# A transformer block in split precision: feature sums for two token tiles at a time in three buffers, one turn copied out of PSUM by ScalarE, and x loaded one item later

## The chip, the cores and the metric

The kernel runs on one core of a Trainium2 chip. The metric is the device time of one execution in microseconds; before the change its median over three runs is 1921.93 us (1920.83 to 1922.19). Engines are named as in the profile: PE (TensorE matmul) and PEld (its weight loads), DVE (VectorE), ACT (ScalarE), POOL (GpSimd) and SP (SyncE, which here only issues DMAs).

## What is computed

One pre-layer-norm block on x of 2048 tokens by 1024 channels, in float32, with 32 heads of 32 channels. Attention is linear, with learned softmax features:

```
h  = x + A(layernorm(x));  out = h + relu(layernorm(h) @ w1) @ w2

q, k, v = heads of layernorm(x) @ wqkv
phi_q = concat(softmax(q @ w_phi), softmax(-(q @ w_phi)))      # 64 features per head
phi_k = concat(softmax(k @ w_phi), softmax(-(k @ w_phi)))
kv = phi_k^T @ v;  z = sum over tokens of phi_k
A  = (phi_q @ kv) / (phi_q . z + 1e-6) @ wo
```

## The kernel before, in words

**Split precision.** Every large product is made of three matmuls, high by high, high by low and low by high (`mm3`, lines 180 to 183), on operands split into a high part (ACT, line 124 for weights) and a low part (DVE or POOL, line 128). PE takes four or eight such steps per item.

**The order.** The work is a list of items (`items`). Between the steps of the items, other functions run at fixed places: `do(n, k, f)` puts f behind step k of item n, `when(step, f)` behind a step counted through. Each function then adds its instructions to the queues of the engines that it names; an engine works through its own queue in that order, and what an instruction needs from another engine it waits for. So one late instruction holds all that stands behind it on its engine. The stages follow each other as: keys and values, queries, output product (`wo`), first MLP product (`up`), second one (`down`).

**The stretch around the change** is that from about 570 to 840 us: the last query items and the 32 items of the output product. Beside them runs the attention, in 32 units of four token tiles and eight heads (`UNITS`, line 524). For a unit u:

- `at_load` (528) loads the exponentials of the features, four tiles by 256 elements, into a tile `qe` (four buffers, two units of a pair in work and two ahead).
- `at_sums` (556): POOL multiplies them by the key sums z into `ez`, a tile of 128x1024 with one buffer (line 559).
- `at_reduce` (563): DVE sums `ez` over the features into `qtz` (line 565).
- `at_den` (571, POOL, lines 574 and 578), `at_inverse` (580, DVE, line 581) and `at_scale` (583, POOL, lines 591 and 596) make the features' scale and apply it.
- `at_turn` (599): DVE transposes in blocks (line 602).
- `at_num` (605), for two units at once: PE multiplies with the key-value sums into four PSUM banks, two named `tp` and two named `ac` (128 small matmuls, line 616); ACT copies them out as high parts (line 623), and `at_low` (632) has DVE make the low parts (line 634), with which the banks come free. The output product reads the result `oT`.

**Layer norm of h**, also beside the output product: `ln_pair` (675) takes two token tiles through nine stages. Stage 1 has DVE's statistics (line 220), stage 2 three POOL steps (229 to 231), stage 3 ACT's scaling (237). Stages 4, 5 and 6 turn a half tile each with four transposes on PE into a `tp` bank (line 244), which ACT copies out (246). Stage 7 turns the last half (line 697) into a `tp` bank, and DVE reads that bank twice, for a sum (698) and a difference (699). In stage 8, POOL makes two more differences (704, 705). `ln_store` sends seven halves off. This runs for b = 0 (four pairs, beside the output product) and for b = 1 (four pairs, beside the MLP).

**PSUM.** There are eight banks: four `mm`, two `tp`, two `ac`. The `tp` banks are handed out in turn, so that the four turns of a layer norm pair use them alternately, and the next `at_num` needs both.

**The residual.** `wo_load` (639) loads a half tile of x into `xh` (five buffers) two items before the item n that needs it (line 1030); `wo_add` (666) adds the product in place, `wo_store` (669) sends it off as h.

Of the kernel before, what the change touches and what calls it, by code (L numbers as in the profile page):

```python
# [9 lines left out]
F32 = mybir.dt.float32  # L10
F32R = mybir.dt.float32r
AF = mybir.ActivationFunctionType
ALU = mybir.AluOpType
AX = mybir.AxisListType

P = 128
S = 2048
D = 1024
H = 32
DH = 32  # L20
# [119 lines left out]
def kernel(  # L140
# [12 lines left out]
    v, act, pool, pe, sp = nc.vector, nc.scalar, nc.gpsimd, nc.tensor, nc.sync  # L153
# [12 lines left out]
    def tp_bank():  # L166
        return psum.tile([P, 512], F32, name="tp", bufs=2)
# [20 lines left out]
    def do(n, k, f, *args):  # L188
        at[n, k].append((f, args))
# [19 lines left out]
    def ln_load(key, parts):  # L209
        xin[key] = xlp.tile([P, D], F32, name="xl") if key[0] == "x" and key[1] >= HT and key[1] % 4 > 1 else \  # L210
            lnp.tile([P, D], F32, name="xin")
        n = D // len(parts)
        for j, p in enumerate(parts):
            sp.dma_start(xin[key][:, j * n:(j + 1) * n], p)

    def ln_stats(key):
        src = xin[key]
        st = lnp.tile([P, 2, 6], F32, name="st", bufs=4)
        for j in range(2):
            v.bn_stats(out=st[:, j, :], in_=src[:, j * 512:(j + 1) * 512])  # L220
        mv = lnp.tile([P, 2], F32, name="mv", bufs=4)
        v.bn_aggr(out=mv, in_=st)
        xst[key] = mv

    def ln_power(key):

        mv = xst[key]
        sc = scx[:, key[1] - HT, :] if key[0] == "s" else lnp.tile([P, 2], F32, name="sc", bufs=4)
        pool.tensor_scalar_add(sc[:, 0:1], mv[:, 1:2], LN_EPS)
        pool.tensor_tensor(out=sc[:, 0:1], in0=sc[:, 0:1], in1=half, op=ALU.pow)  # L230
        pool.tensor_scalar(sc[:, 1:2], mv[:, 0:1], sc[:, 0:1], -1.0, op0=ALU.mult, op1=ALU.mult)
        xst[key] = sc

    def ln_norm(key):
        sc, src = xst.pop(("s", key[1]) if key[0] == "x" and key[1] >= HT else key), xin.pop(key)
        xnt[key] = src if key[0] == "h" else fp_ln.tile([P, D], F32, name="xn")
        act.activation(xnt[key], src, AF.Identity, bias=sc[:, 1:2], scale=sc[:, 0:1])

    def ln_turn(key, j, dst=None):

        xn = xnt[key]
        pt = tp_bank().rearrange("p (k n) -> p k n", k=4)
        for k in range(4):
            pe.transpose(pt[:, k, :], xn[:, (4 * j + k) * P:(4 * j + k + 1) * P], ident)  # L244
        if dst is None:
            act.activation(xn[:, j * 512:(j + 1) * 512], pt.rearrange("p k n -> p (k n)"), AF.Copy)
            return
        d = dst()
        split(d[:, 0, 4 * j:4 * j + 4, :], d[:, 1, 4 * j:4 * j + 4, :], pt)
        if j == 1:  # L250
            del xnt[key]
# [269 lines left out]
    e_q, ez_of, tz_of, den_of, ph_of, acc_of, phT_of = {}, {}, {}, {}, {}, {}, {}  # L521
# [32 lines left out]
                           in1=den.rearrange("p (i h) -> p i h", i=4)[:, :, :, None].to_broadcast([P, 4, 4, 2]))  # L554

    def at_sums(u):
        b, q, r = UNITS[u]
        ez = ap_.tile([P, D], F32, name="ez", bufs=1).rearrange("p (i n) -> p i n", i=4)
        pool.tensor_tensor(out=ez, in0=e_q[u].rearrange("p (i h) s f -> p i (h s f)", i=4),  # L559
                           in1=zb[:, q, None, 256 * r:256 * (r + 1)].to_broadcast([P, 4, 256]), op=ALU.mult)  # L560
        ez_of[u] = ez

    def at_reduce(u):
        tz_of[u] = tz = ap_.tile([P, 32], F32, name="qtz", bufs=2)
        v.tensor_reduce(out=tz, in_=ez_of.pop(u).rearrange("p i (h f) -> p (i h) f", f=DH), op=ALU.add, axis=AX.X)

    def sm_half(u):
        b, q, r = UNITS[u]
# [68 lines left out]
    xh, wo_ps = {}, {}  # L637

    def wo_load(t, hf):
        xh[t, hf] = hp.tile([P, 512], F32, name="xh", bufs=5)  # L640
        sp.dma_start(xh[t, hf], x[t * P:(t + 1) * P, hf * 512:(hf + 1) * 512])

    def wo_item(t, hf, keys):
# [31 lines left out]
    def ln_pair(b, i, stage):  # L675

        keys = [("h", HT * b + 4 * r + i) for r in range(2)]
        if stage == 0:
            for key in keys:
                ln_load(key, [hd[key[1]]])  # L680
        elif stage == 1:
            for key in keys:
                ln_stats(key)
        elif stage == 2:
            for key in keys:
                ln_power(key)
        elif stage == 3:
            for key in keys:
                ln_norm(key)
        elif stage in (4, 5, 6):  # L690
            ln_turn(keys[stage // 6], stage != 4)
        elif stage == 7:
            x1, x2 = (xnt[key] for key in keys)
            s12 = (mp or hp).tile([P, 2, 512], F32, name="s12", bufs=1)
            pt = tp_bank()
            for k in range(4):
                pe.transpose(pt[:, k * P:(k + 1) * P], x2[:, k * P:(k + 1) * P], ident)
            v.tensor_add(s12[:, 0, :], pt, x2[:, 512:])
            v.tensor_sub(x2[:, 0:512], x1[:, 0:512], pt)
            sums[b, i] = s12  # L700
        elif stage == 8:
            x1, s12 = xnt[keys[0]], sums[b, i]
            s4 = (mp or hp).tile([P, 512], F32, name="s4l", bufs=1)
            pool.tensor_tensor(out=s12[:, 1, :], in0=s12[:, 0, :], in1=x1[:, 0:512], op=ALU.subtract)
            pool.tensor_tensor(out=s4, in0=x1[:, 512:], in1=s12[:, 1, :], op=ALU.subtract)
            sums[b, i] = s12, s4
# [127 lines left out]
    def item(gen, *args, keys):  # L834
        items.append((gen, args + (keys,)))
        steps.extend((k,) for k in keys)
        return len(items) - 1
# [10 lines left out]
    wo_first = len(items)  # L848
    for b, tiles in enumerate(groups):
        for hf in range(2):  # L850

            pairs = b == 0 and hf == 0
            for j in range(0, 4, 2 if pairs else 1):
# [3 lines left out]
                for half in range(2):  # L857
                    n = item(wo_pair, tiles[j:j + 2], hf, half, keys=[("wo", hf, 4 * half + k // 2) for k in range(8)])
# [26 lines left out]
    def when(step, f, *args):  # L885

        if step < 8 * first_up:
            do(step // 8, step % 8, f, *args)
        else:
            do(first_up + (step - 8 * first_up) // 4, step % 4, f, *args)  # L890
# [4 lines left out]
    for t in range(1, NT):  # L895
        n = t - 1 if t < HT else q_n[1, t - HT] + 1
# [25 lines left out]
    for n in range(1, 32):  # L922
        for k in ((6,) if n < 8 and n not in (3, 4, 5) else (2, 6)):
            if not todo:
                break
            p, kk = todo.pop(0)
# [68 lines left out]
    zb = kvL = smq = xlp = ap_ = hp = mp = dp = None  # L995
# [13 lines left out]
    for u in range(32):  # L1009
        start = 8 * (a0 + u) if u >= 8 else 8 * (last_kv + 4) + 19 * u // 2  # L1010
        slack = 6 if u < 6 else 0

        stages = (-8, 6, 10, 13, 16, 19, 25) if u < 12 else (7, 14, 18, 20, 22, 24, 28) if u % 2 == 0 else \
            (-1, 9, 13, 15, 17, 19, 23)
        for step, f in zip(stages, (at_load, at_sums, at_reduce, at_den, at_inverse, at_scale, at_turn)):
            if u >= EARLY or f in (at_load, at_scale, at_turn):
                when(max(start + step, 8 * (last_kv + 4)), f, u)
        if u % 2:
            when(start + 30 + slack, at_num, u)
            when(start + 32 + slack, at_low, u)  # L1020
        if u < EARLY:
            start = 8 * (kv_n[1, u // 2, NT - 1] + 4 + 4 * (u % 2))
            for step, f in ((0, early_load), (9, early_sums), (14, early_reduce), (16, at_den), (18, at_inverse),
                            (20, early_scale)):
                when(start + step, f, u)
# [1 line left out]

    order = sorted(wo_n.items(), key=lambda kv: kv[1])
    for (t, hf), n in order:
        do(max(n - 2, wo_first), -1, wo_load, t, hf)  # L1030
        when(8 * n + (11 if n < wo_first + 2 else 9), wo_add, t, hf)
        when(8 * n + (10 if n > order[-3][1] else 14), wo_store, t, hf)

# [5 lines left out]
    for i in range(4):  # L1039
        for stage in range(9):  # L1040
            when(wo0 + 64 + 40 * i + LN2[0][stage], ln_pair, 0, i, stage)
            when(up0 + 60 + 68 * i + LN2[1][stage], ln_pair, 1, i, stage)
        for j in range(7):
            when(wo0 + 64 + 40 * i + LN2[0][9] + j // 2, ln_store, 0, i, j)
            when(up0 + 60 + 68 * i + LN2[1][9] + j, ln_store, 1, i, j)
# [37 lines left out]
    for b in range(2):  # L1083
        for m in DOWN:
            n = down_n[b, m, NP - 1] + 1
            name, more = {1: "x1", 5: "x4", 6: "x2", 4: "x3"}.get(m), \
# [33 lines left out]
    for i in range(4):  # L1120
        r = slice(32 * i, 32 * (i + 1))
# [76 lines left out]
```

## Time and profile before

| | |
|---|---|
| median of three runs | 1921.93 us |
| the profiled execution | 1921.28 us |
| its span, from the first to the last instruction | 1919.4 us |
| mean granted TensorE clock | 0.997 |
| busy: PE, DVE, POOL, ACT | 1896.9, 1026.5, 967.6, 756.3 us |
| DMA, mean rate | 225 GB/s |

How to read it: the profile is of one execution. A row of the timeline has the start, the duration, engine, line, operation, output and inputs; in square brackets stands how long the engine was idle before it, and who ended that. A row of the waits has who waited for whom, the total, the number of times and the longest. A busy engine is not one at its peak: matmuls overlap each other, so the pace of PE is read from the distance between the starts of two of them.

### The profile page before, as it was taken

What the parts mean: (1) busy time and instruction counts of PE and PEld (TensorE: products, weight loads), DVE (VectorE), ACT (ScalarE), POOL (GpSimd) and SP (SyncE); (2) the same over time, 40 slices, a digit from 0 to 9 for tenths busy, and PEclk for the clock granted to TensorE, in tenths of its full rate; (3) what the DMA queues carried; (4) which work ended last, traced back from release to release, by engine and by line L of the source; (5) the groups of instructions that cost most, each with busy time, mean ns of one, the idle gap of its engine ahead of it and who ended that gap; (6) DMA issues with size and microseconds to landing.
All of it is one profiled execution on the core that took longest, in us unless ns stands there. A gap on an engine that the chain in (4) does not pass through costs nothing.

```text
span 1919.4 us, 31405 instructions
## 1 busy us (share of the span) xinstructions
PE 1896.9 (99%) x11416; PEld 1561.6 (81%) x11416; DVE 1026.5 (53%) x1631; ACT 756.3 (39%) x1310; POOL 967.6 (50%) x935
## 2 busy tenths in 40 slices
PE   9999999999999999999999999999999999999998
PEld 7888788877778777788888888888888888888887
DVE  6666578767679766545544564344433433343333
ACT  5433326222223112245444564444444444444442
POOL 4777752789955877423343322222244444444443
PEclk9999999999999999999999999999999999999999
DMA  6888786666665656697787897666677677777775
GB/s 219 276 264 271 231 275 198 209 196 211 192 218 182 204 206 235 204 285 225 247 265 237 255 295 221 187 185 193 212 243 226 191 240 233 242 212 220 215 216 170
DMA packets 292699, 432.15 MB, mean 225 GB/s; under 512 B 24384, under 2 KB 150336, under 8 KB 292544
## 3 DMA queue, kind: packets, MB, share of 16 engines
q1 hardware_dynamic: 275648, 413.36, 68.4%
q10 hardware_dynamic: 16896, 16.78, 2.6%
q8 instruction: 90, 1.47, 0.3%
q14 instruction: 65, 0.53, 0.1%
HBM read 292.68 MB, written 137.36 MB: 224 GB/s over the span
## 4 chain that ended last, share of the span: by engine, by line
PE 81%; POOL 10%; DMA 4%; issue 2%; DVE 2%; ACT 0%; SPq 0%; POOLq 0%; ACTq 0%; DVEq 0%
PE mm L181 20%; PE mm L182 20%; PE mm L183 20%; PE ac L183 4%; PE ac L182 4%; PE ac L181 4%; POOL b L350 2%; PE tp L183 2%; PE tp L181 2%; PE tp L182 2%; POOL ez L559 2%; POOL w L128 2%; DMA b<-in_w_dram 2%; DMA t<-b 1%; PE tp L244 1%
## 5 line engine op out<-in xcount | busy, mean ns | idle before, releaser
L128 POOL TENSOR_TENSOR w<-raw,w 128x512 fp32r<-128x512 f32 x355 | 472.1, 1332 | 726.5 <-ACT w L124 683.5
L124 ACT ACTIVATE w<-raw 128x512 fp32r<-128x512 f32 x686 | 409.4, 626 | 517.8 <-PE mm L183 253.8
L128 DVE TENSOR_TENSOR w<-raw,w 128x512 fp32r<-128x512 f32 x331 | 268.3, 811 | 530.9 <-ACT w L124 530.4
L181 PE MATMUL mm<-w,xT 128*128 128x512 f32 x768 | 311.0, 405 | 0.0
L182 PE MATMUL mm<-w,xT 128*128 128x512 f32 x768 | 300.5, 391 | 3.8 <-POOL w L128 3.3
L183 PE MATMUL mm<-w,xT 128*128 128x512 f32 x768 | 299.8, 390 | 0.0
L181 PE MATMUL mm<-hT,w 128*128 128x512 f32 x672 | 262.6, 391 | 0.0
L183 PE MATMUL mm<-hT,w 128*128 128x512 f32 x672 | 261.6, 389 | 0.0
L182 PE MATMUL mm<-hT,w 128*128 128x512 f32 x672 | 261.5, 389 | 0.0
L350 POOL TENSOR_TENSOR b<-b 128x256 f32<-128x256 f32 x224 | 183.9, 821 | 90.3 <-DMA b<-in_w_dram 77.8
L182 PEld LDWEIGHTS mm<-w,xT 128*128 128x128 f32 x768 | 144.6, 188 | 34.5 <-POOL w L128 5.6
L181 PEld LDWEIGHTS mm<-w,xT 128*128 128x128 f32 x768 | 144.4, 188 | 30.6 <-issue 1.8
L183 PEld LDWEIGHTS mm<-w,xT 128*128 128x128 f32 x768 | 144.2, 188 | 30.7
L181 PE MATMUL mm<-w 128*128 128x512 f32 x392 | 152.5, 389 | 0.0
L182 PE MATMUL mm<-w 128*128 128x512 f32 x392 | 152.5, 389 | 0.0
L183 PE MATMUL mm<-w 128*128 128x512 f32 x392 | 152.5, 389 | 0.0
L183 PEld LDWEIGHTS mm<-hT,w 128*128 128x128 f32 x672 | 126.2, 188 | 26.2
L181 PEld LDWEIGHTS mm<-hT,w 128*128 128x128 f32 x672 | 126.2, 188 | 25.9
L182 PEld LDWEIGHTS mm<-hT,w 128*128 128x128 f32 x672 | 126.2, 188 | 25.7
L182 PEld LDWEIGHTS mm<-w 128*128 128x128 f32 x392 | 73.6, 188 | 15.3
L181 PEld LDWEIGHTS mm<-w 128*128 128x128 f32 x392 | 73.6, 188 | 15.2
L183 PEld LDWEIGHTS mm<-w 128*128 128x128 f32 x392 | 73.6, 188 | 15.2
(161 smaller groups left out, 3139.4 us busy)
## 6 DMA issues: line engine op xcount, KB each, us to landing
raw<-t SPq DMA_DIRECT2D x224, 256.0 KB, 3.9
raw<-ad SPq DMA_DIRECT2D x196, 256.0 KB, 3.0
raw<-in_w_dram SPq DMA_DIRECT2D x168, 256.0 KB, 3.1
b<-in_w_dram SPq DMA_DIRECT2D x56, 512.0 KB, 4.2
t<-b SPq DMA_DIRECT2D x56, 512.0 KB, 4.2
ad<-c SPq DMA_DIRECT2D x112, 256.0 KB, 3.6
ad<-s SPq DMA_DIRECT2D x84, 256.0 KB, 4.2
ed<-qe ACTq DMA_DIRECT2D x32, 512.0 KB, 4.5
```

Source lines behind the costliest of these rows:

```text
L124: nc.scalar.activation(w[:, 0, :], raw[1], AF.Copy)
L128: eng.tensor_tensor(out=w[:, 1, :], in0=raw[1], in1=w[:, 0, :].bitcast(F32), op=ALU.subtract)
L181: pe.matmul(ps, a_hi, b_hi, start=first, stop=False, skip_group_check=more)
L182: pe.matmul(ps, a_hi, b_lo, start=False, stop=False, skip_group_check=more)
L183: pe.matmul(ps, a_lo, b_hi, start=False, stop=last, skip_group_check=more)
L244: pe.transpose(pt[:, k, :], xn[:, (4 * j + k) * P:(4 * j + k + 1) * P], ident)
L350: pool.tensor_tensor(out=tsum[j, *out], in0=tsum[j, *a], in1=tsum[j, *b], op=ALU.subtract)
L559: pool.tensor_tensor(out=ez, in0=e_q[u].rearrange("p (i h) s f -> p i (h s f)", i=4), in1=zb[:, q, None, 256 * r:256 * (r + 1)].to_broadca ...
```

## The change

It has four parts. `at_sums` and `at_reduce` work on two tiles at a time: two products of 128x512 and two sums, where there was one of each on 128x1024. The product's buffers are two halves in the attention's pool, and from the output product on (when the pool `hp` is open) each third half goes to a third buffer in `hp`; the room for it comes from `xh`, which has four buffers in place of five. `wo_load` runs one item before its use in place of two. In stage 7 of `ln_pair`, for b = 0 alone, ACT first copies the turned half from its bank to a place that stage 8 overwrites later, and both DVE operations read the copy.

```diff
     def at_sums(u):
+
         b, q, r = UNITS[u]
-        ez = ap_.tile([P, D], F32, name="ez", bufs=1).rearrange("p (i n) -> p i n", i=4)
-        pool.tensor_tensor(out=ez, in0=e_q[u].rearrange("p (i h) s f -> p i (h s f)", i=4),
-                           in1=zb[:, q, None, 256 * r:256 * (r + 1)].to_broadcast([P, 4, 256]), op=ALU.mult)
-        ez_of[u] = ez
+        for j in range(2):
+            third = hp is not None and (2 * u + j) % 3 == 2
+            ez_of[u, j] = ez = (hp if third else ap_).tile([P, 2, 256], F32, name="ez", bufs=1 if third else 2)
+            pool.tensor_tensor(out=ez, in0=e_q[u].rearrange("p (i h) s f -> p i (h s f)", i=4)[:, 2 * j:2 * j + 2, :],
+                               in1=zb[:, q, None, 256 * r:256 * (r + 1)].to_broadcast([P, 2, 256]), op=ALU.mult)
 
     def at_reduce(u):
         tz_of[u] = tz = ap_.tile([P, 32], F32, name="qtz", bufs=2)
-        v.tensor_reduce(out=tz, in_=ez_of.pop(u).rearrange("p i (h f) -> p (i h) f", f=DH), op=ALU.add, axis=AX.X)
+        for j in range(2):
+            v.tensor_reduce(out=tz[:, 16 * j:16 * (j + 1)], in_=ez_of.pop((u, j)).rearrange("p i (h f) -> p (i h) f", f=DH),
+                            op=ALU.add, axis=AX.X)
...
     def wo_load(t, hf):
-        xh[t, hf] = hp.tile([P, 512], F32, name="xh", bufs=5)
+        xh[t, hf] = hp.tile([P, 512], F32, name="xh", bufs=4)
...
             pt = tp_bank()
             for k in range(4):
                 pe.transpose(pt[:, k * P:(k + 1) * P], x2[:, k * P:(k + 1) * P], ident)
+            if b == 0:
+                act.activation(s12[:, 1, :], pt, AF.Copy)
+                pt = s12[:, 1, :]
             v.tensor_add(s12[:, 0, :], pt, x2[:, 512:])
             v.tensor_sub(x2[:, 0:512], x1[:, 0:512], pt)
...
     for (t, hf), n in order:
-        do(max(n - 2, wo_first), -1, wo_load, t, hf)
+        do(max(n - 1, wo_first), -1, wo_load, t, hf)
```

How the queues change is shown at three places. The line numbers behind the changed functions are a few higher after the change (602 becomes 606, 616 becomes 620, 667 becomes 671).

DVE, beside the output product, around stage 7 of the first layer norm pair (`s` is its tile of sums); before the change:

```order
L602 STREAM_TRANSPOSE qe<-qe 128x1024 x2
L667 TENSOR_TENSOR xh<-mm,xh 128x512
L565 TENSOR_REDUCE qtz<-ez 128x32
L698 TENSOR_TENSOR s_7885<-tp,xin 128x512
L699 TENSOR_TENSOR xin<-xin,tp 128x512
L565 TENSOR_REDUCE qtz<-ez 128x32
L581 RECIPROCAL qden<-qden 128x16
L634 TENSOR_TENSOR oT<-tp,oT 128x8x32 x2
```

The same place after the change:

```order
L606 STREAM_TRANSPOSE qe<-qe 128x1024 x2
L671 TENSOR_TENSOR xh<-mm,xh 128x512
L568 TENSOR_REDUCE qtz<-ez 128x16 x2
L705 TENSOR_TENSOR s_7930<-s_7930,xin 128x512
L706 TENSOR_TENSOR xin<-xin,s_7930 128x512
L568 TENSOR_REDUCE qtz<-ez 128x16 x2
L585 RECIPROCAL qden<-qden 128x16
L638 TENSOR_TENSOR oT<-tp,oT 128x8x32 x2
```

Nothing has changed places; each reduction is two, and the sum and the difference of stage 7 read `s` in SBUF where they read the bank `tp`.

ACT at the same stage, after the change (before it, the row of L703 is not there and the others follow each other alike):

```order
L237 ACTIVATE xin<-xin,sc 128x1024 x2
L246 ACTIVATE xin<-tp 128x512 x3
L703 ACTIVATE s_7930<-tp 128x512
L627 ACTIVATE oT<-tp 128x8x32 x2
L627 ACTIVATE oT<-ac 128x8x32 x2
```

The new copy stands behind the three copies of the other turns and ahead of the copies that follow the next `at_num`.

SP, at the first items of the output product, where `raw` is a weight block, `xh` the residual and `qe` a unit's features; before and after:

```order
L641 DMA xh<-in_x_dram 128x512 x2
L320 DMA raw<-in_wo_dram 128x512 x3
L641 DMA xh<-in_x_dram 128x512 x2
L320 DMA raw<-in_wo_dram 128x512
L530 DMA qe<-ed_81 128x1024 x2
L641 DMA xh<-in_x_dram 128x512
```

```order
L645 DMA xh<-in_x_dram 128x512 x2
L320 DMA raw<-in_wo_dram 128x512 x4
L530 DMA qe<-ed_81 128x1024 x2
L645 DMA xh<-in_x_dram 128x512 x2
```

The second two loads of x now stand behind the last weight block and two units of features. Further on, one load of x stands at each item as before, for the next item in place of the one after it.

## The prediction

> **What bounds the kernel now.** I read the page first (busy shares), then who waits on PE, then PE's order of time around those waits.
>
> ```profile
> PE 1896.9 (99%) x11416; PEld 1561.6 (81%) x11416; DVE 1026.5 (53%) x1631; ACT 756.3 (39%) x1310; POOL 967.6 (50%) x935
> ```
>
> ```profile
> PE tp L616 <- DVE xin L699: 5.8, 2, 3.3
> PE mm L182 <- POOL w L128: 3.3, 3, 1.4
> PE tp L244 <- ACT xn L237: 2.8, 2, 2.7
> PE tp L244 <- DVE oT L634: 1.2, 1, 1.2
> ```
>
> PE is busy for 99% of the span: the kernel can win only what PE idles, and what PE runs slowly after it. The waits are few. The first and the last of the four lie in the stretch that the change touches: twice the small matmuls of the attention wait for DVE's second reading of the layer norm's last turned half (L699), and once a turn waits for the attention's low parts (L634). The other two are at other places.
>
> ```profile
> 700.00:740.00 40.00, 35.48 (x515) 28.57 (x508) 24.53 (x43) 7.96 (x17) 32.74 (x38) 0.96 0.68 232
> 780.00:830.00 50.00, 50.00 (x343) 41.12 (x342) 22.48 (x34) 12.84 (x20) 15.15 (x19) 0.97 0.77 243
> ```
>
> These windows give the busy time of PE, PEld, DVE, ACT and POOL, then the granted clock. PE lacks 4.5 us in the first; in the second it is always busy, but at a clock of 0.97: a stall is paid a second time, in matmuls that run slowly behind it. What each costs is read from PE's starts:
>
> ```profile
> 699.71 0.42 PE L616 MATMUL tp<-qe,kvL 32*32 32x128 f32 x8
> ...
> 703.47 0.31 PE L616 MATMUL tp<-qe,kvL 32*32 32x128 f32 x4 [3.34 <-DVE xin L699]
> ...
> 706.28 0.63 PE L182 MATMUL mm<-w,oT 128*128 128x512 f32 x1
> ...
> 707.93 0.39 PE L183 MATMUL mm<-w,oT 128*128 128x512 f32 x1
> ...
> 717.27 0.39 PE L182 MATMUL mm<-wf,oT 128*128 128x512 f32 x1
> 717.49 0.39 PE L183 MATMUL mm<-wf,oT 128*128 128x512 f32 x1
> 717.81 0.34 PE L616 MATMUL tp<-qe,kvL 32*32 32x128 f32 x8
> ...
> 719.98 0.40 PE L182 MATMUL mm<-wf,oT 128*128 128x512 f32 x1
> ...
> 735.42 0.44 PE L244 MATMUL tp<-ident,xin 128*128 128x128 f32 x2 [1.18 <-DVE oT L634]
> ...
> 774.59 0.42 PE L616 MATMUL tp<-qe,kvL 32*32 32x128 f32 x8
> ...
> 777.47 0.31 PE L616 MATMUL tp<-qe,kvL 32*32 32x128 f32 x4 [2.46 <-DVE xin L699]
> ...
> 779.57 0.63 PE L182 MATMUL mm<-wf,oT 128*128 128x512 f32 x1
> 780.00 0.63 PE L183 MATMUL mm<-wf,oT 128*128 128x512 f32 x1
> ...
> 782.97 0.40 PE L181 MATMUL mm<-wf,oT 128*128 128x512 f32 x1
> ```
>
> An undisturbed group is the one at 717.81: 2.17 us from its first small matmul to the second full one at 719.98. At full clock, full matmuls start 0.22 us apart (717.27, 717.49); I use 0.227, the third of a 0.68 us step. **Stall A**, at 699.71, takes 6.57 us to 706.28, which is 4.40 more than 2.17; the four starts from there to 707.93 take 1.65 in place of 0.91, 0.74 more. A costs 5.14. **Stall C**, at 774.59, takes 4.98 to 779.57, 2.81 more; the eight starts to 782.97 are some 0.43 apart (3.40 in place of 1.82), 1.58 more. C costs 4.39. **Stall B** at 735.42 costs its 1.18; no slow matmuls stand behind it. Together 10.71 us.
>
> The tail behind C is weighed by itself. In the trace, an idle time of 2.46 us was enough for half-rate matmuls behind it. The Trainium skill, "TensorE: Matmul & The Clock Gate", section "What's actually happening", has the clock fall only after at least one idle window of about 3.4 us. By that rule C would have no tail, and the sum would be 1.58 smaller; the trace shows it, so it stays in.
>
> **The change, part by part.**
>
> *The copy by ACT (stage 7).* What holds A and C is seen on DVE:
>
> ```profile
> 698.59 1.25 DVE L602 STREAM_TRANSPOSE qe<-qe 128x1024 f32<-128x1024 f32 x1 [0.95 <-POOL qe L596]
> ...
> 700.92 1.22 DVE L565 TENSOR_REDUCE qtz<-ez 128x32 f32<-128x1024 f32 x1 [0.51 <-POOL ez L559]
> ...
> 702.65 0.68 DVE L699 TENSOR_TENSOR xin<-xin,tp 128x512 f32<-128x512 f32 x1
> ...
> 772.56 1.25 DVE L602 STREAM_TRANSPOSE qe<-qe 128x1024 f32<-128x1024 f32 x1 [0.95 <-POOL qe L596]
> ```
>
> ```profile
> L246 ACT ACTIVATE xin<-tp x24: 577/600/605, 694.8 to 1057.4; 128x512 f32<-128x512 f32 x24
> ```
>
> In A, the bank is full before 699 and is read only at 702.65, behind a reduction that waits for POOL. After the change ACT reads it, at 0.60 us like the three turns before it, and ACT is busy for 7.96 us of 40 there: the bank is free long before 703. What is late next is the features' transposes: 698.59 + 1.25 = 699.84, against the group's start at 699.71, so nothing is left to wait for; in C 773.81, against 774.59, 0.78 us to spare. I take both stalls as gone: minus 9.53. But PE then comes 5.14 + 1.18 = 6.32 us earlier to C, and the 0.78 are not enough unless the chain of the features gets faster, by 5.54 us.
>
> *The products in halves.*
>
> ```profile
> 657.53 2.38 POOL L559 TENSOR_TENSOR ez<-qe,zb 128x1024 f32<-128x1024 f32 x1
> ...
> 727.55 2.41 POOL L559 TENSOR_TENSOR ez<-qe,zb 128x1024 f32<-128x1024 f32 x1
> 731.30 2.37 POOL L559 TENSOR_TENSOR ez<-qe,zb 128x1024 f32<-128x1024 f32 x1 [1.33 <-DVE qtz L565]
> ...
> 772.49 2.40 POOL L559 TENSOR_TENSOR ez<-qe,zb 128x1024 f32<-128x1024 f32 x1
> ```
>
> ```profile
> L704 POOL TENSOR_TENSOR s<-s,xin x8: 1279/1293/1750, 705.0 to 1060.1; 128x512 f32<-128x512 f32 x8
> L565 DVE TENSOR_REDUCE qtz<-ez 128x32 f32<-128x1024 f32 x24 | 29.1, 1214 | 31.3 <-POOL ez L559 31.2
> L503 DVE TENSOR_REDUCE qmx<-mm 128x16 f32<-128x512 f32 x2 | 1.3, 674 | 0.0
> ```
>
> From 657.53 to 772.49 stand the products of nine pairs. A pair takes 731.30 + 2.37 - 727.55 = 6.12 us: the second product waits 1.33 for the sum of the first, since there is one buffer. With three half buffers POOL's four halves follow each other: the fourth needs the buffer of the first, summed two halves ago. A half is not in the trace. From below it is half of 2.39, 1.20; from above the slowest product of its size, 1.75 (L704). I take the middle of that row, 1.29, the same size and number of inputs. A pair is then 5.16, 0.96 less, and nine pairs 8.6 less, more than the 5.54 that C needs, so the transposes stay ahead of PE. At 1.20 a pair wins 1.32; at 1.75 it loses 0.88. On DVE a half sum costs between 0.61 (half of 1.214) and 0.67 (L503); the last one ends 0.55 earlier behind its product, at a cost of 0.1 us or less per unit, hidden since DVE is busy for 24.5 of 40 us.
>
> For B both count: DVE's low parts stand behind the pair's last sum, which comes 0.96 + 0.55 = 1.51 us earlier, against a stall of 1.18. Minus 1.18; its other end is nothing.
>
> *Two inputs from SBUF.* L698 and L699 read PSUM and SBUF today, 0.68 us each. With both inputs in SBUF beside POOL, the nearest rows are DVE's weight splits:
>
> ```profile
> 647.52 3.48 DVE L128 TENSOR_TENSOR wf<-raw,wf 128x512 fp32r<-128x512 f32 x2
> ```
>
> That is 1.74 each. The two may cost DVE up to 2.1 us more for each of the first four layer norm pairs, from below nothing; I take the whole. Behind them stand the second unit's sums and the low parts. PE asks for those only at its next group, at 717.81 on the old scale; cost nothing, and up to 1 us if that cover is gone.
>
> *x one item later.* The order that DVE adds in is kept; a load now starts where the next item's load started.
>
> ```profile
> 824.12 0.64 SPq L641 DMA_DIRECT2D xh<-in_x_dram  x1
> ```
>
> ```profile
> 833.46 0.68 DVE L667 TENSOR_TENSOR xh<-mm,xh 128x512 f32<-128x512 f32 x1
> ```
>
> This is the tightest place, since the load at 824.12 stands at the place where the one for this addition will: 9.3 us are left. The longest landing of a load of x in this trace took 7.6:
>
> ```profile
> DMA to landing us min/median/max: 2.5/5.1/7.6
> ```
>
> One buffer less and one item later leave the distance to the store ahead as it is. Cost nothing; were a load late, DVE would wait, and PE only once all four banks of the products are full.
>
> *Earlier POOL stage.* Around 575 to 660 us, where units are not yet in pairs on POOL, halves add 4 x 1.29 - 2 x 2.39 = 0.38 us per pair and remove little waiting; the transposes there are hardly ahead of PE. I put plus 0.3 there, between 0 and 1.
>
> **The sum.** 1921.28 (the profiled execution) - 9.53 - 1.18 + 0.3 = 1910.9. The median of the runs is 0.65 above the profiled one, so I forecast 1911.5 for the median. Its own range: 1910 (no cost for the halves, and runs spread by 0.6) to 1913.5 (B stays, and 0.8 for halves and DVE).
>
> **The rivals.**
>
> *The transposes take the place of the bank.* If a half costs 1.53, a pair takes 6.12 as before, and POOL's chain is not faster. A is won, but at C the transposes still end at 773.81, and PE, there since 768.27, waits 5.5 us for them. It goes on at 773.81 where it went on at 777.47: 3.7 us are won, all told, with the same tail: 1918.2. For it: C's margin of only 0.78. Against: the middle of the row of L704 is 1.29.
>
> *The halves slow POOL down: slower than before.* If the sums that now run beside POOL's products hold these up, a half may cost 1.75, the slowest of its size. Then a pair costs 7.0, 0.88 more, and nine pairs 7.9 more. The transposes of C end at 773.81 + 7.9 = 781.7, and PE goes on there 4.2 us later than at 777.47, with A's gain used up by the longer wait: 1926.1. It decides from where nine pairs lose 3.66 us, 0.41 each: a half of 1.63. Against it: the products of 657.53 to 772.49 took 2.4 us beside other work of DVE. The Trainium skill, "SBUF — State Buffer", section "Who interferes with whom", says that a DVE reduction never contends with GpSimd, and that an operation with two SBUF inputs does. By that rule this rival falls away, and only the two DVE operations of stage 7 collide; L128's row agrees with the second half of it.
>
> *The bank stays held.* If the copy stood behind something late on ACT, PE would wait for ACT in place of DVE: no gain but B's, 1920.7. Against it: ACT's idle time.
>
> **How the numbers follow.** Forecast 0.72; transposes 0.12; bank held 0.09; slower 0.07. The range runs from 1909.5 to 1918.2: the forecast's own, half a microsecond lower for the spread of the runs, and up to the first rival, since without it more than 2 in 10 would be left out. A measurement of this kernel can tell about 0.2%, 3.8 us, from no change, so faster means under 1918.1: the forecast and half of the first rival, 0.78; within 0.2%: its other half and the bank, 0.15; slower 0.07.
>
> **What will show it.** Right: no wait of L616 for the stage 7 operations, and a clock of 1.00 in the windows up to 830; products in halves of 1.2 to 1.3 us that follow each other without 1.33 us of idle time; the turn that was at 735.42 without a wait. Wrong: PE waiting for L602's transposes (now line 606), halves over 1.5 us, or a new wait of PE between 570 and 840 us of more than 1 us; then the sum above fails by that wait and its tail.

## The result and the profile after

The changed kernel takes 1911.59 us (median of six runs, 1909.82 to 1914.57), and the kernel before takes 1921.76 on the same chip: a ratio of 0.9949, 95% interval 0.9936 to 0.9962. The profiled execution took 1909.82, with a span of 1907.8. The forecast was 1911.5 for the median. The time came out, but one of its reasons did not, as the experiments show.

The waits of PE after the change (who waited for whom: total, times, longest, in us):

```profile
PE mm L182 <- POOL w L128: 2.9, 4, 1.4
PE tp L244 <- ACT xn L237: 1.8, 1, 1.8
...
PE mm L182 <- DVE hT L741: 1.3, 1, 1.3
...
PE tp L620 <- POOL ez L562: 0.4, 1, 0.4
```

The waits for stage 7 and for the low parts are gone. A new one of 1.3 us, for `hT`, the input of the MLP's first product, comes later, at 851.80. The windows of the same stretches (busy PE, PEld, DVE, ACT, POOL, then clock, DMA share, GB/s):

```profile
700.00:740.00 40.00, 40.00 (x509) 32.27 (x495) 27.52 (x51) 8.53 (x18) 35.95 (x45) 1.00 0.81 269
...
780.00:830.00 50.00, 50.00 (x349) 41.17 (x349) 24.86 (x33) 17.44 (x26) 14.09 (x13) 1.00 0.88 278
```

PE has no gap left in the first (it lacked 4.5 us), and the clock is 1.00 in both (it was 0.96 and 0.97). PE's starts at the places of stalls A and C:

```profile
698.91 0.34 PE L620 MATMUL tp<-qe,kvL 32*32 32x128 f32 x8
...
700.74 0.50 PE L181 MATMUL mm<-w,oT 128*128 128x512 f32 x1
701.08 0.39 PE L182 MATMUL mm<-w,oT 128*128 128x512 f32 x1
...
711.85 0.34 PE L620 MATMUL tp<-qe,kvL 32*32 32x128 f32 x8
...
724.79 0.34 PE L620 MATMUL tp<-qe,kvL 32*32 32x128 f32 x8
...
739.74 0.34 PE L620 MATMUL tp<-qe,kvL 32*32 32x128 f32 x8
...
767.44 0.34 PE L620 MATMUL tp<-qe,kvL 32*32 32x128 f32 x8
...
780.38 0.34 PE L620 MATMUL tp<-qe,kvL 32*32 32x128 f32 x8
```

From 698.91 the group takes 2.17 us to its second full matmul, the undisturbed value. The next group starts 12.94 us behind it, and 12.94 behind 767.44 too; before, these distances were 18.10 and 17.37. So A gave 5.16 and C 4.43, where 5.14 and 4.39 were forecast. Stall B lay between the two groups that now start at 724.79 and 739.74, 14.95 apart in place of 16.14: 1.19 us less. The group starts of before that the prediction doesn't show:

```profile
730.75 0.34 PE L616 MATMUL tp<-qe,kvL 32*32 32x128 f32 x8
...
746.89 0.34 PE L616 MATMUL tp<-qe,kvL 32*32 32x128 f32 x8
...
791.96 0.34 PE L616 MATMUL tp<-qe,kvL 32*32 32x128 f32 x8
```

What DVE and POOL do at A's place:

```profile
698.79 1.75 DVE L706 TENSOR_TENSOR xin<-xin,s 128x512 f32<-128x512 f32 x1
700.47 1.27 DVE L568 TENSOR_REDUCE qtz<-ez 128x16 f32<-128x512 f32 x2
```

```profile
694.52 5.47 POOL L562 TENSOR_TENSOR ez<-qe,zb 128x512 f32<-128x512 f32 x4
699.96 0.69 POOL L578 TENSOR_TENSOR qtz<-qtz,smq 128x32 f32<-128x32 f32 x1
...
708.45 3.79 POOL L562 TENSOR_TENSOR ez<-qe,zb 128x512 f32<-128x512 f32 x3
```

The four halves of a pair follow each other without idle time, 5.47 us in place of some 6.1, although DVE's difference beside them now takes 1.75 in place of 0.68. DVE begins it at 698.79, before PE's group even starts. That DVE comes this early was the first sign that the copy might not be needed.

### The profile page after: what moved, and what is told of

The parts are those of the page before. It is cut to its first block, busy times and chain, and to the rows that moved or that the text cites. A ratio compares the mean times of both kernels' runs of the same rounds, so it can differ in the third digit from the quotient of the medians.

```text
span 1907.8 us, 31460 instructions
## 1 busy us (share of the span) xinstructions
PE 1894.3 (99%) x11416; PEld 1561.0 (82%) x11416; DVE 1034.8 (54%) x1657; ACT 758.0 (40%) x1314; POOL 974.2 (51%) x961
## 4 chain that ended last, share of the span: by engine, by line
PE 88%; POOL 5%; DMA 4%; issue 1%; DVE 1%; SPq 1%; ACT 0%; POOLq 0%; DVEq 0%; ACTq 0%
PE mm L181 22%; PE mm L182 22%; PE mm L183 22%; PE ac L181 4%; PE ac L182 4%; PE ac L183 4%; PE tp L182 2%; PE tp L183 2%; PE tp L181 2%; POOL b L350 2%; POOL w L128 2%; PE tp L244 1%; PE tp L278 1%; DMA b<-in_w_dram 1%; DMA t<-b 1%
```

## The experiments

All twelve were timed in five rounds against the kernel before on the same chip. Ratios are to that kernel, with 95% intervals. The intervals reach about 0.001 to either side.

**The copy by ACT alone**, added to the kernel before:

```diff
+            if b == 0:
+                act.activation(s12[:, 1, :], pt, AF.Copy)
+                pt = s12[:, 1, :]
```

> Before, with ACT's copy of the last turned half (b = 0) alone; products whole, one buffer, x as before. Theory (the copy frees the bank, the halves make the features' chain fast enough): the waits for L699 go, but with 6.1 us a pair the transposes become late behind the won time: 1.2 us at the pair after A, and at C (774 us on the scale of before) PE waits some 5 us for the transposes; the 1.2 us at the turn (B) stay. 1917 to 1918.5 us. Rival (the copy does it all): no wait for transposes over 0.5 us, 1912 to 1913 us.

1922.03 us, ratio 1.0015 (1.0006 to 1.0024): nothing is won, and both theories missed the time. PE's waits there:

```profile
715.00 0.34 PE L616 MATMUL tp<-qe,kvL 32*32 32x128 f32 x8 [1.64 <-DVE qe L602]
...
736.36 1.05 PE L244 MATMUL tp<-ident,xin 128*128 128x128 f32 x4 [3.85 <-DVE oT L634]
...
792.83 0.34 PE L616 MATMUL tp<-qe,kvL 32*32 32x128 f32 x8 [1.64 <-DVE qe L602]
```

A and C are gone, so the copy does what it says. But PE then arrives early at the next things that the same chain makes. At the pair behind A and at the pair behind C it waits 1.64 us each for the transposes, and B has grown from 1.18 to 3.85. The theory had the transposes right in kind, though it looked for some 5 us of them at C itself, and it left B at 1.2. Why PE waits is seen on POOL:

```profile
698.68 2.38 POOL L559 TENSOR_TENSOR ez<-qe,zb 128x1024 f32<-128x1024 f32 x1
702.40 2.78 POOL L559 TENSOR_TENSOR ez<-qe,zb 128x1024 f32<-128x1024 f32 x1 [1.33 <-DVE qtz L565]
705.15 0.70 POOL L574 TENSOR_TENSOR qtz<-qtz,smq 128x32 f32<-128x32 f32 x1
...
713.62 2.35 POOL L559 TENSOR_TENSOR ez<-qe,zb 128x1024 f32<-128x1024 f32 x1
```

From one pair's first product to the next pair's, POOL takes 713.62 - 698.68 = 14.94 us where PE, unhindered, takes 12.94. I call this distance the **round** of POOL. Before the change it was 712.53 - 698.51 = 14.02:

```profile
698.51 2.37 POOL L559 TENSOR_TENSOR ez<-qe,zb 128x1024 f32<-128x1024 f32 x1
...
712.53 2.41 POOL L559 TENSOR_TENSOR ez<-qe,zb 128x1024 f32<-128x1024 f32 x1
```

The copy itself makes it longer, since DVE's difference with both inputs in SBUF and POOL's work hold each other up: POOL's second product takes 2.78 in place of 2.36, its next step 0.70 in place of 0.26, and DVE's difference 2.90 in place of 0.68.

```profile
702.83 2.90 DVE L702 TENSOR_TENSOR xin<-xin,s 128x512 f32<-128x512 f32 x1
```

PE loses to POOL what it no longer loses to the bank.

**Halves alone**, the change without those three lines (the third buffer and x's later load stay):

> The changed kernel without ACT's copy: halves, third buffer and x one item later stay. Theory of the prediction, taken strictly (A and C need the copy): PE still waits 2 to 3 us for DVE's second reading of the bank at A and C, 1919 to 1921 us. Rival (the halves alone bring DVE's readings early enough, since in the changed kernel DVE comes to stage 7 at 697.7 us, before the group at 698.9): waits under 0.5 us there, B gone, 1911 to 1913 us; then copy and halves are two remedies for the same stall.

1910.5 us, ratio 0.9947 (0.9935 to 0.9960): the whole gain, as the rival had it. DVE and POOL at A's place:

```profile
699.04 0.68 DVE L703 TENSOR_TENSOR xin<-xin,tp 128x512 f32<-128x512 f32 x1
```

```profile
695.25 5.03 POOL L562 TENSOR_TENSOR ez<-qe,zb 128x512 f32<-128x512 f32 x4
...
708.27 3.80 POOL L562 TENSOR_TENSOR ez<-qe,zb 128x512 f32<-128x512 f32 x3
```

The difference starts at 699.04 in place of 702.65, and PE waits only 0.7 us for the bank, where it waited 3.34. The round is 13.02.

**x's loads alone**, four buffers and one item later:

```diff
-        xh[t, hf] = hp.tile([P, 512], F32, name="xh", bufs=5)
+        xh[t, hf] = hp.tile([P, 512], F32, name="xh", bufs=4)
...
-        do(max(n - 2, wo_first), -1, wo_load, t, hf)
+        do(max(n - 1, wo_first), -1, wo_load, t, hf)
```

> Before, with four buffers for x and its load one item before the use. Theory: costs nothing, 1921.8 us, within 1 us. Rival (the later loads crowd the stretch before the MLP, where the changed kernel has a new wait of 1.3 us at 851.8 us): the same new wait at that place and 1.3 to 2 us more than before.

1922.85 us, ratio 1.0008 (0.9999 to 1.0017): no effect on the time, as forecast. In the trace there is one. The first two loads of features into `qe` now stand ahead of two loads of x that stood before them, and POOL waits less for the features; before, and in this run:

```profile
643.98 2.37 POOL L559 TENSOR_TENSOR ez<-qe,zb 128x1024 f32<-128x1024 f32 x1 [2.91 <-DMA qe<-ed]
```

```profile
643.41 2.40 POOL L559 TENSOR_TENSOR ez<-qe,zb 128x1024 f32<-128x1024 f32 x1 [0.56 <-DMA qe<-ed]
```

From the group of small matmuls next to this place to the one at A, PE takes 700.21 - 646.59 = 53.62 us, where it took 699.71 - 644.79 = 54.92. The same holds for all fourteen traces shown or named here: in the eight with x's later load POOL waits 0.4 to 0.7 us and PE takes 53.58 to 53.72; in the six with x as before they are 2.4 to 3.4 and 54.36 to 56.44. In this run the 1.3 us don't show in the time; B, for one, has grown to 2.63.

**The change with the copy for three tiles of each four** (`if b == 0 and i < 3`):

> The changed kernel with the copy for the first three layer norm pairs of b = 0 only; the fourth has no group of the attention behind it. Theory: the fourth copy makes POOL's two differences, and with them the stores and loads of the MLP's input, 1 to 2 us late, which is the new wait of 1.3 us at 851.8 us; without it that wait goes: 1910 us, 1.4 us under the changed kernel. Rival (the wait comes from x one item later): no change against the changed kernel, 1911.6 us.

1909.57 us, ratio 0.9943 (0.9931 to 0.9956). PE does not wait for `hT` in this trace, as the theory had it; the repeats below take that back. Its ratio is not distinguishable from the change's.

**Two half buffers**, no third one; x as in the kernel before, no copy:

```diff
-            third = hp is not None and (2 * u + j) % 3 == 2
-            ez_of[u, j] = ez = (hp if third else ap_).tile([P, 2, 256], F32, name="ez", bufs=1 if third else 2)
+            ez_of[u, j] = ez = ap_.tile([P, 2, 256], F32, name="ez", bufs=2)
```

> Products and sums in halves with two half buffers (as much memory as one whole product took), five buffers for x with its loads where they were, no copy by ACT. Theory 'overlap': what wins is that a half's sum (0.68 us on DVE) runs beside the next half's product (1.29 on POOL); with two buffers the third half needs the buffer of the first, which is summed while the second is made, so two buffers are enough: 1909.5 to 1912, and a pair's four products take 5.0 to 5.5 us from first start to last end. Rival 'third buffer': DVE stands at x's addition (0.65) or at layer norm's two operations (1.36) when a half is ready, and POOL then waits for it at each pair; with up to 1.0 us a pair in place of 0.9 to 1.0 won, the gain is lost: 1917 to 1922, and POOL's idle time before the products for the sums is at 15 us or more, where the halves with three buffers have 8.

1916.52 us, ratio 0.9977 (0.9965 to 0.9988): less than half of the gain, between the two theories. The pair at A is as fast as with three (5.08 us), so overlap needs only two. What is lost at A is one half of head start, at a place ahead of it where DVE turns to layer norm's statistics:

```profile
679.44 2.55 POOL L561 TENSOR_TENSOR ez<-qe,zb 128x512 f32<-128x512 f32 x2
686.95 2.55 POOL L561 TENSOR_TENSOR ez<-qe,zb 128x512 f32<-128x512 f32 x2 [4.96 <-DVE qtz L567]
...
697.52 5.08 POOL L561 TENSOR_TENSOR ez<-qe,zb 128x512 f32<-128x512 f32 x4
```

With two buffers POOL makes two halves and waits; with three, only the fourth half was left to make (in the halves alone):

```profile
685.94 1.30 POOL L562 TENSOR_TENSOR ez<-qe,zb 128x512 f32<-128x512 f32 x1 [4.99 <-DVE qtz L568]
```

The pair ends there at 687.2 in place of 689.5, and A's difference starts 2.3 us earlier. PE's waits for it with two buffers, at A and at C, are 2.04 and 1.60 us. This run also has x's loads as before; by the distance above, 54.64 in place of 53.62, they cost it some 1 us ahead of A.

**Two half buffers with the copy for three of four tiles:**

> Two half buffers, x as before, and the copy by ACT for the first three turned tiles of each layer norm set (as in the earlier run with three buffers, 1909.57). If the copy is worth the 0.7 us that PE waits for layer norm at the third pair in the halves alone, and two buffers are enough: 1909 to 1911. If the copy only trades that wait for slower POOL work (two SBUF inputs on DVE): as e5 within 0.1%.

1912.18 us, ratio 0.9957 (0.9944 to 0.9971). Here the copy is worth 4.3 us (against 1916.52): the waits of 2.04 and 1.60 us that two buffers leave at stage 7 are gone. Neither theory had that.

**One half of each pair made twice** (three buffers, no copy):

```diff
+            for again in range(2 if u % 2 == 0 and j == 0 else 1):
+                pool.tensor_tensor(out=ez, ...)
```

> The halves alone (three buffers, no copy), and the first half of each pair's first unit is made twice on POOL (1.27 us more for a pair, the same result). Theory 'POOL's time for a pair sets the transposes': a pair takes 5.03 + 1.27 = 6.3 us, 0.2 more than the 6.07 of whole products, so the transposes and DVE's order behind them are as late as before and PE waits again for layer norm's operations at the third and sixth pair: 1918 to 1923. Rival 'the last sum': what PE waited for hung on how soon a unit's last sum ends behind its product (0.68 in place of 1.21) or on DVE's own time, and POOL has idle time to spare: 1909.5 to 1913.

1920.31 us, ratio 0.9996 (0.9985 to 1.0007): all of the gain is gone, by 1.27 us on POOL for each pair. Both stalls for stage 7 are back:

```profile
PE tp L621 <- DVE xin L704: 6.0, 2, 3.3
```

```profile
696.31 6.33 POOL L563 TENSOR_TENSOR ez<-qe,zb 128x512 f32<-128x512 f32 x5
...
710.59 6.40 POOL L563 TENSOR_TENSOR ez<-qe,zb 128x512 f32<-128x512 f32 x5
```

The five take 6.33 us, and the round is 14.28. The third buffer, x's later load and the sums in halves are all still there. So POOL's time for a pair carries the gain; the shorter last sum alone does not.

**The product alone in halves**, one whole buffer, one whole sum:

```diff
+        for j in range(2):
+            pool.tensor_tensor(out=ez[:, 2 * j:2 * j + 2, :], ...)
```

> The kernel before, with the product alone in two halves, into the one whole buffer, and one whole sum; no copy. Theory 'overlap': without a second buffer and without sums in halves no sum runs beside a product of the same pair, so nothing is won and 2 x 1.29 - 2.39 = 0.2 us a unit is lost on POOL: 1920 to 1925, with the 1.33 us waits of the second product as before. Rival 'size': products of half the size suit POOL and DVE better by themselves (less held by each other), and a good part of the 10 us comes without the overlap: below 1917.

1924.43 us, ratio 1.0015 (1.0006 to 1.0024). The second product waits 1.33 us for the sum as before, and PE waits 7.0 us for stage 7. Small products by themselves win nothing; the sum must run beside the next product.

**The copy, with stage 8 taken from POOL** (ACT copies one input each, and the two subtractions are left out); whole products:

```diff
-            pool.tensor_tensor(out=s12[:, 1, :], in0=s12[:, 0, :], in1=x1[:, 0:512], op=ALU.subtract)
-            pool.tensor_tensor(out=s4, in0=x1[:, 512:], in1=s12[:, 1, :], op=ALU.subtract)
+            act.activation(s12[:, 1, :], s12[:, 0, :], AF.Copy)
+            act.activation(s4, x1[:, 512:], AF.Copy)
```

> The kernel before with the copy by ACT (which alone gained nothing), and layer norm's two operations of stage 8 taken from POOL: ACT copies one input in place of each subtraction (the subtractions are left out). Whole products, one buffer. Theory 'POOL's chain takes over': the copy alone failed because POOL's work for a unit pair with a layer norm step takes 14.9 us against PE's 12.9; without 2.6 us of it the chain is down to 12.3, the copy's gain stays, and neither the transposes nor the low parts hold PE for more than 1.5 us each: 1910 to 1914. Rival 'contention': the copy fails since DVE's operations with two SBUF inputs (2.9 us beside POOL) push the low parts late by themselves: these stay, and the time stays at 1917 or more.

1917.6 us, ratio 0.9982 (0.9973 to 0.9991): both theories missed. PE and POOL:

```profile
734.62 0.69 PE L244 MATMUL tp<-ident,xin 128*128 128x128 f32 x2 [5.10 <-DVE oT L634]
```

```profile
698.68 2.38 POOL L559 TENSOR_TENSOR ez<-qe,zb 128x1024 f32<-128x1024 f32 x1
...
711.83 2.38 POOL L559 TENSOR_TENSOR ez<-qe,zb 128x1024 f32<-128x1024 f32 x1
...
726.82 2.38 POOL L559 TENSOR_TENSOR ez<-qe,zb 128x1024 f32<-128x1024 f32 x1
```

With a round of 711.83 - 698.68 = 13.15 PE no longer stalls for the transposes. But I had looked at one round only. The next has stage 2 (six small POOL steps, 724.30 to 726.82) in place of stage 8, and takes 726.82 - 711.83 = 14.99. DVE's low parts start at 734.21, right behind the last sum of the pair that begins there, and hold PE for 5.10 us: stall B at over four times its size. This is POOL's chain once more, at the next place. The slow difference is in the trace too (2.88 us, at 702.84), one round earlier; there POOL loses the 0.8 us by which 13.15 is above the 12.3 expected, so the rival had a part of it.

**The change, the halves alone and the copy for three, once more**, on one chip:

> The changed kernel once more, beside the halves alone on the same chip. If the copy is worth nothing on top of the halves with three buffers: within 0.1% of the halves alone (1909.5 to 1912.5 both). If the copy's cost on POOL (two SBUF inputs beside it) shows in the time: 1 us or more above the halves alone. Within the trace, POOL's 43 halves have a mean above that of the halves alone by 0.02 us or more.

> Halves in three buffers without the copy, once more, for the comparison with the changed kernel: 1909.5 to 1912.5, with PE waiting for layer norm's second operation at the third pair (0.7 us in the first run) and for nothing else of stage 7.

> The changed kernel with the copy for three of the four turned tiles of each set, once more: 1909 to 1912. If PE's new wait before the MLP (1.3 us in the changed kernel, absent here in the first run) comes of the fourth tile's copy, it is absent here again and present in the changed kernel of the same chip; if it comes and goes with the run, one of the two differs from its first run.

1910.54, 1911.58 and 1909.12 us; ratios 0.9947 (0.9935 to 0.9959), 0.9951 (0.9937 to 0.9966) and 0.9941 (0.9929 to 0.9952). The intervals lie in each other. The cost on POOL is there as expected: 36 halves between 655 and 800 us have a mean of 1.315 us with the copy and 1.288 without. It does not show in the time. The wait for `hT` was 1.2 us in the change, 0.6 with the copy for three (none in its first run), and none in the halves alone (0.7 in their first run). So it comes and goes with the run, and also without the fourth tile's copy. It was longest in the two traces that have this copy, and whether the copy lengthens it stays open. The expectation for the halves alone, a wait of 0.7 us for stage 7 at the third pair, missed: there is none there, and one of 0.2 at C. No version tried beats the change by more than can be measured.

## Why the prediction was right, and where it was wrong

**The sum of the stalls: right.** 5.14, 1.18 and 4.39 were forecast; the distances of the groups became 5.16, 1.19 and 4.43 us shorter, tails and all.

**"I take both stalls as gone: minus 9.53", put down to the copy: wrong.** The failed step is the reading of "What holds A and C": the bank was read late, and I let ACT read it. It was late because DVE stood behind a reduction that waited for POOL. In the halves alone DVE comes there 3.6 us earlier, and that is enough: they have the whole gain, the copy alone has none. The prediction did say that C needs the chain to be 5.54 us faster, but it kept the halves as a condition of the copy's gain, not as its source. The first rival says what the copy is worth on a chain that is not faster, 1918.2; measured alone it was 1922.03. The rival counted neither the growth of B nor what the copy costs POOL, both of which are in that run's trace. What the runs show for each combination (ratio to the kernel before on the same chip, first run of each; the first two rows have x as before, the third has it one item later):

| products | no copy | with copy |
|---|---|---|
| whole, one buffer | 1 | 1.0015 |
| halves, two buffers | 0.9977 | 0.9957 (three tiles of four) |
| halves, three buffers | 0.9947 | 0.9949; 0.9943 (three of four) |

**"The products in halves": right in mechanism, with corrections.** A pair without the copy takes 5.03 us (5.16 forecast), and the pad of 1.27 us a pair takes all of the gain back: as the rivals had it, the price of the half decides. But "nine pairs 8.6" is not how the lead comes about. The ninth pair starts at 772.49, when C's last transpose (772.56) is about to start, so eight stand ahead of it. A round without layer norm on POOL gained more than 0.96: from 12.34 us (657.53 to 669.87) it went to 10.72 (656.14 to 666.86), since POOL also waits 0.30 us for the pair's last sum in place of 0.83, which I had counted for B alone. And at layer norm's statistics POOL waits for DVE whatever it has gained (3.47 us at 688.11 before, 3.86 at 685.24 after): after the change DVE itself waits there for the tiles of h to be loaded, and a part of the lead is lost each time.

```profile
681.69 1.29 DVE L220 BATCH_NORM_STATS2 st<-xin 128x6 f32<-128x512 f32 x2 [1.50 <-DMA xin<-hd]
...
694.60 1.25 DVE L606 STREAM_TRANSPOSE qe<-qe 128x1024 f32<-128x1024 f32 x1 [0.95 <-POOL qe L600]
...
765.24 1.25 DVE L606 STREAM_TRANSPOSE qe<-qe 128x1024 f32<-128x1024 f32 x1 [0.95 <-POOL qe L600]
```

The transposes of A ended at 695.85, 4.0 us earlier, and those of C at 766.49, 7.3 earlier. That was enough for C, with 0.95 us to spare. And the third buffer was used in the prediction only to say that the halves follow each other. Three buffers and x's later load together are worth some 6 us without the copy (0.9977 to 0.9947); by the traces about 1 us of that is x's, and the rest lies at A and C, where the half counts that a third buffer has ready.

**"Two inputs from SBUF": the cost was sought on DVE alone.** DVE's part was within bounds in the change:

```profile
L706 DVE TENSOR_TENSOR xin<-xin,s 128x512 f32<-128x512 f32 x4 | 4.9, 1226 | 0.0
L705 DVE TENSOR_TENSOR s<-s,xin 128x512 f32<-128x512 f32 x4 | 3.7, 923 | 4.2 <-ACT s L703 4.2
```

Together 0.8 us more than the 1.36 of the two before. But POOL pays as well, which the term left out: the four halves take 5.47 in place of 5.03, and a step of 0.26 behind them 0.69. The round is 708.45 - 694.52 = 13.93 with the copy and 13.02 without. The rule of the Trainium skill that the second rival cites ("SBUF — State Buffer", section "Who interferes with whom") fits on both sides: the reductions beside the products cost these nothing (5.03 us for four, where two without a sum beside them took 2.51 in the run with the product alone in halves), and the operations with two SBUF inputs do collide. With the copy the last transpose for the group at 780.38 ends at 780.43, 0.27 us ahead of the first matmul that reads it (780.70); in the change's second trace it ends 1.2 us ahead of the group's start, in the halves alone 3.2. The change's round at A, 13.93, is still longer than PE's 12.94: it costs nothing because the transposes come to A with a lead of 3.1 us, where before they had none. In the first trace this cost is hidden by a hair.

**Stall B, minus 1.18: right in this trace, on a thin margin.** It was 0.7 us again in the change's second trace, and 0.6 and none in the two of the halves alone.

**"Earlier POOL stage", plus 0.3: right, at 0.2.** The groups from 573.62 to 644.79 took 71.17 us; after the change, from 573.92 to 645.29, they take 71.37. The runs with products in halves have 71.3 to 71.4 here (but for the one with a half made twice), the others 71.2. From there to A the groups came 1.3 us nearer to each other. The run with x's loads alone has the same 1.3, so that comes of the later load of x and not of the halves.

**x one item later at nothing: right for the time of its own run, wrong for PE.** It was weighed by the load that comes late, and not by the features that come early: worth 1.3 us of PE's time ahead of A in the change's trace. **The new wait at 851.80** was outside the stretch that I watched (570 to 840 us). It cost 1.3 to 1.4 us in the change's two traces. That it comes from layer norm's halves being ready later, seen from an earlier PE, is a reading of the traces and was not tested; what decides it stays open.

The time came out because the sum was taken from PE's stalls, all of which went; which part of the change earned them did not enter it. Two things that the sum left out, 1.3 us won ahead of A and 1.3 lost at 851.80, cancelled in this trace; that was luck.

## What to carry to other kernels

A bank, a transpose and a low part that are late one after the other may be late from the same chain: before giving one of them a way round, compare the time that the chain takes for a round (here POOL's 14.02 us) with that of the engine that waits (12.94). If the chain is longer and has no lead at the start of that round, the way round moves the wait on. Then what shortens the chain wins: here splitting a step so that its consumer runs beside it, with one buffer more for the place where the consumer is away. One round is not all: a round of 13.93 was harmless behind a lead of 3.1 us, and one of 13.15 won little since the next took 14.99. When two parts of a change each seem to explain a gain, price each one without the other.

## What was unexpected in the hardware

The slow matmuls behind a stall don't follow from the length of the wait alone. In the copy's run, waits of 1.64 us at 715.00 and 792.83 were followed by full matmuls 0.43 us apart, for some 3 us:

```profile
717.66 0.63 PE L183 MATMUL mm<-wf,oT 128*128 128x512 f32 x1
718.09 0.63 PE L181 MATMUL mm<-w,oT 128*128 128x512 f32 x1
```

In the run with x's loads alone, a wait of 2.31 us at 702.93 had none behind it:

```profile
705.02 0.39 PE L182 MATMUL mm<-w,oT 128*128 128x512 f32 x1
705.26 0.40 PE L183 MATMUL mm<-w,oT 128*128 128x512 f32 x1
```

Waits of 1.1 to 1.2 us in these stretches had none either. So the tail (up to 1.7 us here) is a part of a stall's price that a prediction can only bound. The collision of an operation with two SBUF inputs beside POOL also went beyond my upper row: 2.90 us beside a whole product, where the row of weight splits gave 1.74; beside halves it was at most 1.78.
